# Transposes in place of identity matmuls, a range check moved to VectorE, and norm products half a step later, in an attention and expert-layer kernel

## The chip, the core and the metric

The kernel runs on one core of a Trainium2 chip. The metric is the device time of one execution in microseconds (us). Five engines work side by side, each on its own list of instructions in a fixed order: TensorE (PE in the profile; PEld are its weight loads), VectorE (DVE), ScalarE (ACT), GpSimd (POOL) and SyncE (SP), which issues the transfers. They wait for one another through semaphores.

## The reference

Attention through 32 memory slots per head, and behind it a layer that is applied to every token:

```python
a = softmax(phi, axis=seq)                      # (8, 8, 576, 32)
k_m = einsum('bhsm,bhsd->bhmd', a, k)           # 32 keys and 32 values a head
v_m = einsum('bhsm,bhsd->bhmd', a, v)
attn = softmax(q @ k_m.T / sqrt(64))            # (8, 8, 576, 32)
x = (attn @ v_m) as (4608 tokens, 512)
h = x @ w_in                                    # 512 -> 2048
out = (h - tanh(h)) @ w_out                     # 2048 -> 512
```

The two weights arrive as 64-bit floats, the rest as 32-bit floats.

## The kernel before, in words

**Layer.** The 4608 tokens are cut into 18 units of 256 tokens, and the 2048 hidden columns into four blocks of 512. A slot is one unit and one block. The script writes slots 18 to 71 out in a loop over `(u, fb)`: `u142` in the lists of instructions is the tile `u` of unit 14, block 2 (slot 58). TensorE first makes the slot's hidden values, `hs`, by 24 matmuls (`mm1`, L563). They go through ACT (`u`, L570), VectorE (`h`, L578), ACT (`u`, L583), VectorE (`h`, L588) and ACT (`g`, L594); POOL makes the low part of `g` (L599), and one slot later VectorE adds forms of it, `f` (L612). TensorE multiplies g and f of the block that lies two slots back with W_out (`mm2`, L699 and L706), into the tiles `x` and `o`. At the end of a unit (slots 21, 25 and so on to 57, 61, 65, 69) `evict` empties them on VectorE: r at L759, L760, L761, L764 and L771. The next unit's first product into x waits for the second of these, L760. `hs` and the tile of PSUM that the small products share (tag "pa": psc, ptr, pkv, pp, pno, pni) exist once each.

**Attention.** Its steps for batches 3 to 7 are words in tables (PLAN, PLAN3) that give the slot and the place in it: ahead of the `u` of L583 (`do(0)`), behind mm2 (`do(1)`, after a ";") or at the slot's end (`do(2)`, after a "|"). Batches 0 to 2 run in the 18 blocks ahead of slot 18, while W_in and W_out are still coming in and being split into two 16-bit parts. A batch's turn (`turn`, word U) takes the averaged keys and values `kvn` (`norm`, word N) to `ptr` by products with an identity matrix; ACT copies kT (L264) and vh (L487) out of it, and VectorE makes vl (L489). `expo_turn` turns the exponentials of batches 0 and 1 in the same way (`pet`, `pel`). `pp` (L515) are the values times W_in; ACT (L528) and VectorE (L533) take it to `ph`, the weights of mm1.

**Range check.** The 16-bit arithmetic holds for weights in a certain range. The words of PLAN_C check them as the layer runs: CE and CQ load one of 32 pieces of raw weights again (`chk`, 128x512 of 64 bits, 512 KB), into a buffer of another tile (e, q); CW (`window`) checks its high halves, which lie two words apart: POOL squares them (L439, `fy`) and ACT sums the result of a Relu of 1 - 2^30 y (L443), which is zero if all are large enough. CW, CE, CQ and SI, SO words of `do(0)` are put in `due` and run after POOL's g. SI, SO (ACT) and SS (VectorE L452, L453, tiles sqi, sqo) square and add the split weights; NI and NO (`norms_out`: TensorE L473, `pno`; ACT L474, `wn`) sum over partitions. Slot 68 judges all sums (`good`, `grow`), and `pgood` takes the verdict to a branch at the end, to a second kernel for other ranges, which is not taken with these inputs.

The program's order on each engine is the order of the script (`in_order`), so a table's words alone set which instruction stands behind which.

Of the kernel before, what the change touches and what calls it, by code (L numbers as in the profile page):

```python
# [8 lines left out]
F32 = mybir.dt.float32  # L9
# [4 lines left out]
AF = mybir.ActivationFunctionType  # L14
ALU = mybir.AluOpType
AX = mybir.AxisListType
PSUM = bass.MemoryType.PSUM

P = 128
B, H, S, D, NM = 8, 8, 576, 64, 32  # L20
# [19 lines left out]
CW = (  # L40
    0.33333331252017, -0.13333128520786, 0.053934788850892, -0.021660115374759,
    0.0082189218977914, -0.0025104593252184, 0.000420695493864,
)
# [6 lines left out]
N_F1 = 32  # L50
# [36 lines left out]
class Attention:  # L87
# [105 lines left out]
    def expo_turn(self, b, d, ps, ps_tail):  # L193

        nc, pt = self.tc.nc, d["pt"]
        pa, pb = self.psum(f"pet{b}", ps), ps_tail.tile([P, 512], F32, tag="o1", name=f"pel{b}")
        pe = pa.rearrange("p a x -> p (a x)").rearrange("p (c x) -> p c x", x=P)
        for c in range(4):
            for r in range(2):
                nc.tensor.matmul(pe[:, 2 * c + r], pt[:, r, P * c : P * c + P], self.c["ident"], start=True, stop=True)  # L200
        for r in range(2):
            nc.tensor.matmul(pb[64 * r : 64 * r + 64, 0:P], pt[:, r, 512:S], self.c["ident"], start=True, stop=True)
        yield
        d["e"] = self.big.tile([P, 9, 128], F32, tag="e", name=f"e{b}", bufs=1)
        nc.scalar.activation(d["e"][:, 0:8], pe, AF.Copy)
        nc.scalar.activation(d["e"][:, 8], pb[:, 0:P], AF.Copy)

    def pool(self, b, d):
        self.pool_half(b, d, 0)
# [20 lines left out]
    def norm(self, b, d):  # L230
        nc, big, pa = self.tc.nc, self.big, d["pk"]
        r = big.tile([P, 2], F32, tag="kr", name=f"kr{b}")
        nc.vector.tensor_scalar(r, pa[:, :, 128], EPS, None, op0=ALU.add)
        nc.vector.reciprocal(r, r)
        kvn = big.tile([P, 2, 128], F32, tag="kvn", name=f"kvn{b}")
        nc.vector.tensor_tensor(
            kvn, pa[:, :, 0:128], r.unsqueeze(2).to_broadcast((P, 2, 128)), op=ALU.mult
        )
        d["kvn"] = kvn

    def norm_half(self, b, d, r):
        nc, big, pa = self.tc.nc, self.big, d["pk"]
        if r == 0:
            d["kvn"] = big.tile([P, 2, 128], F32, tag="kvn", name=f"kvn{b}")
        z = big.tile([P, 2], F32, tag="kr", name=f"kr{b}{r}")[:, 0:1]
        nc.vector.tensor_scalar(z, pa[:, r, 128:129], EPS, None, op0=ALU.add)
        nc.vector.reciprocal(z, z)
        nc.vector.tensor_scalar(d["kvn"][:, r], pa[:, r, 0:128], z, None, op0=ALU.mult)

    def turn(self, b, d, ps=None):  # L250

        nc = self.tc.nc
        kvn = d["kvn"]
        pa = self.psum(f"ptr{b}", ps)
        for i in range(2):
            for r in range(2):
                nc.tensor.matmul(
                    pa[64 * r : 64 * r + 64, i, 0:128], kvn[:, r, 64 * i : 64 * i + 64], self.c["ident"],
                    start=True, stop=True,
                )  # L260
        d["pt"] = pa
        yield
        d["kT"] = self.big.tile([P, 128], F32, tag="kT", name=f"kT{b}", bufs=1)
        nc.scalar.activation(d["kT"], pa[:, 0, 0:128], AF.Copy)  # L264
# [73 lines left out]
def split_path(ctx, tc, c, ins, out):  # L338
    nc = tc.nc
    w_in, w_out = ins["w_in"], ins["w_out"]  # L340
    stat = c["stat"]
    const = ctx.enter_context(tc.tile_pool(name="wts", bufs=1))
    big = ctx.enter_context(tc.tile_pool(name="big", bufs=2))
# [91 lines left out]
    def window(k):  # L435

        hf = raws.pop(k).bitcast(F32).rearrange("p (f w) -> p f w", w=2)[:, :, 1]
        y = big.tile([P, 512], F32, tag="ot", name=f"fy{k}")
        nc.gpsimd.tensor_tensor(y, hf, hf, op=ALU.mult)  # L439
        return y, k  # L440

    def window_sum(y, k):
        nc.scalar.activation(y, y, AF.Relu, bias=c["one"], scale=-(2.0 ** 30), accum_out=stat[:, k : k + 1])  # L443

    def squares_in(fb):
        acc["q", fb] = big.tile([P, 4, 512], F16, tag="q" if fb < 3 else "e", name=f"sqi{fb}", bufs=2 if fb < 3 else 1)
# [32 lines left out]
    st = [dict() for _ in range(B)]  # L479
# [11 lines left out]
    def att_window(b):  # L491
        for g in range(2):
            y = big.tile([P, 64], F32, tag="vy", name=f"vy{b}{g}", bufs=1)
            o = N_F1 + 2 * b + g
            nc.scalar.activation(y, st[b]["kvn"][:, g, 64:128], AF.Square, accum_out=stat[:, o : o + 1])

    def att_split(b, t, eng):

# [76 lines left out]
    def g1(u, fb, stay=False):  # L575
        hp, uu = gs[u, fb]
        h3 = hp if stay else big.tile([P, 4, UT], F32, tag="h3", name=f"h3{u}{fb}")
        nc.vector.scalar_tensor_tensor(h3, hp, C2 * S_G / (S_A * S_P), uu, op0=ALU.mult, op1=ALU.mult)  # L578
        gs[u, fb] = (h3, uu)

    def g1_square(u, fb):
        uu = gs[u, fb][1]
        nc.scalar.activation(uu, uu, AF.Square, bias=c["beta"])  # L583
# [237 lines left out]
    def go(word, whole=True):  # L821

        name = word.rstrip("0123456789")
        run = going.pop(word, None) or STEPS[name](*(int(x) for x in word[len(name):]))
        if run is None or not hasattr(run, "send"):
            return
        for _ in run:
            if not whole:
                going[word] = run
                return  # L830

    for word in START.split():
        if ":" in word:
            k, tag = word.split(":")
# [17 lines left out]
    PLAN_C = (  # L852
# [5 lines left out]
    )  # L858
    tasks = {}
# [2 lines left out]
            tasks.setdefault(4 * (b * S // UT) + off, []).append(words.format(b))  # L862
    for sl, words in PLAN_C:
        tasks.setdefault(sl, []).append(words)
    loads, chk, due, squared = list(range(32)), [], [], []

    def borrow(tag):
        chk.append(loads.pop(0))
        load_raw(chk[-1], tag, "chk")

    def step(word, late=False):
        if word[0] == "C" or word[:2] in ("SI", "SO"):
            if not late:
                due.append(word)
            elif word == "CW":
                squared.append(window(chk.pop(0)))
            elif word[0] == "C":
                borrow({"E": "e", "Q": "q", "S": "sc"}[word[1]])
            else:
                go(word)  # L880
        else:
            go(word)
# [4 lines left out]
    for sl, (u, fb) in enumerate(slots, 18):  # L887
        if sl == 18:
            acc["x"] = ps_h.tile([P, 2, 512], F32, tag="h", name="x")
            acc["hp"] = ps_h.tile([P, 4, UT], F32, tag="h", name="hs")  # L890
        todo = ["", "", ""]
        for w in tasks.get(sl, []):
            w, _, todo_2 = w.partition("|")
            w, _, todo_1 = w.partition(";")
            for i, x in enumerate((w, todo_1, todo_2)):
                todo[i] += " " + x

        def do(i):
            for x in todo[i].split():
                step(x)  # L900

        list(mm1(u, fb))
        g1(u, fb)
        do(0)
        g1_square(u, fb)
        a_forms(*forms.pop())
        g2(u, fb)
        queue.append((u, fb))
        v, vb = queue.pop(0)
        mm2_blocks(v, vb, vb == 0, vb == NFB - 1)  # L910
        while squared:
            window_sum(*squared.pop(0))
        do(1)
        g2_high(u, fb)
        g3(u, fb, nc.gpsimd)
        while due:
            step(due.pop(0), True)
        evict()
        forms.append((u, fb))
        do(2)  # L920
# [18 lines left out]
def check(tc, c, big):  # L939
    nc = tc.nc  # L940
    stat = c["stat"]
    good = big.tile([P, N_CHECK], F32, tag="good", name="good", bufs=1)
    nc.vector.tensor_scalar(good[:, 0:N_F1], stat[:, 0:N_F1], 0.0, None, op0=ALU.is_le)
    o = N_F1
    for n, (lo, hi) in ((2 * B, V_WIN), (DF // P, WI_WIN), (DM // P, WO_WIN)):
        s, g = stat[:, o : o + n], good[:, o : o + n]
        nc.vector.tensor_scalar(g, s, lo, None, op0=ALU.is_ge)
        nc.vector.scalar_tensor_tensor(g, s, hi, g, op0=ALU.is_le, op1=ALU.mult)
        o += n
    row = big.tile([P, 1], F32, tag="grow", name="grow", bufs=1)  # L950
    nc.vector.tensor_reduce(row, good, axis=AX.X, op=ALU.add)
    c["row"] = row
# [190 lines left out]
```

## Time and profile before

| | |
|---|---|
| Time, median of 3 runs (lowest to highest) | 666.1 us (665.86 to 666.72) |
| Profiled execution, span from the first to the last instruction | 664.0 us |
| TensorE clock granted, mean | 0.998 |
| Busy: TensorE, VectorE, ACT, POOL | 640.2, 529.2, 374.0, 257.4 us |
| Moved by transfers | 85 MB, 128 GB/s on average |

The median is 2.1 us above the span; the profiled execution's whole time isn't given apart from its span. In the profile a row of a group has the line, engine, operation, output and inputs with their sizes and count, then busy time and the mean of one in nanoseconds, or min/median/max. In a row of the timeline the first two numbers are start and duration in us, and brackets at its end give the idle time of the engine ahead of it and what ended it. One fp32 matmul shows as two records.

### The profile page before, as it was taken

The page shows a single profiled execution, that of the slowest core. Times are in us where ns is not written, and L with a number is a line of the kernel's source. Part 1 is how long each engine was busy: PE and PEld are TensorE (multiplying, and loading weights), DVE is VectorE, ACT ScalarE, POOL GpSimd, SP SyncE. Part 2 cuts the span into 40 slices and gives each one's busy share as a digit, 9 for nine tenths or more (in the row PEclk, how much of TensorE's full clock was granted, in tenths as well). Part 3 has the DMA queues.
Part 4 walks back from the last instruction along what each step waited for, and adds up shares of the span by engine and source line. Part 5 has one row for each costly group of instructions (what it writes and reads, how often), then busy time and mean ns, then how long its engine had stood idle before and what let it go on. Part 6 is the DMA issues. An engine that isn't in the chain of part 4 may idle for free.

```text
span 664.0 us, 15493 instructions
## 1 busy us (share of the span) xinstructions
PE 640.2 (96%) x6630; PEld 454.6 (68%) x6630; DVE 529.2 (80%) x800; ACT 374.0 (56%) x507; POOL 257.4 (39%) x173
## 2 busy tenths in 40 slices
PE   8788999999999999999999999999999989999996
PEld 4364656655557768786767777777776767787785
DVE  6799999999855778875988689877976787868763
ACT  3577576655524556445654565546555566666541
POOL 0224331343112344433545253535352454455521
PEclk9999999999999999999999999999999999999999
DMA  8999344223123402242322433142413342224201
GB/s 341 401 359 380 106 154 148 97 88 129 60 80 101 163 2 98 86 128 105 130 87 96 135 105 113 66 168 71 146 63 136 100 135 88 68 97 135 85 33 38
DMA packets 25996, 84.98 MB, mean 128 GB/s; under 512 B 2880, under 2 KB 2880, under 8 KB 25152
## 3 DMA queue, kind: packets, MB, share of 16 engines
q1 hardware_dynamic: 24624, 81.55, 35.6%
q10 hardware_dynamic: 1296, 2.36, 0.9%
q8 instruction: 54, 0.88, 0.6%
q14 instruction: 22, 0.18, 0.1%
HBM read 72.37 MB, written 11.53 MB: 126 GB/s over the span
## 4 chain that ended last, share of the span: by engine, by line
PE 66%; DVE 16%; DMA 6%; issue 5%; ACT 3%; POOL 2%; SPq 0%; DVEq 0%; ACTq 0%; POOLq 0%
PE hs L563 16%; PE x L706 11%; PE o L699 10%; PE o L706 8%; PE o L642 7%; PE h L563 4%; DMA raw<-in_w_out_dram 3%; PE o1h L642 3%; DVE f L612 3%; PE pp L515 3%; DVE h L588 2%; DVE h L578 2%; DMA kv<-in_kva_dram 2%; PE pkv L220 2%; DVE ph L533 1%
## 5 line engine op out<-in xcount | busy, mean ns | idle before, releaser
L599 POOL TENSOR_TENSOR g<-h,g 128x1024 f16<-128x1024 f32 x67 | 146.6, 2188 | 332.9 <-ACT g L594 216.0
L563 PEld LDWEIGHTS <-ph 128*128 128x128 f16 x2304 | 176.9, 98 | 21.0 <-issue 6.0
L563 PE MATMUL hs<-ah,ph 128*128 128x256 f16 (+3 forms) x1152 | 151.5, 246 | 0.0
L578 DVE SCALAR_TENSOR_TENSOR h<-hs,u 128x1024 f32<-128x1024 f32 x54 | 65.8, 1218 | 89.1 <-ACT u L570 89.1
L594 ACT ACTIVATE g<-h 128x1024 f16<-128x1024 f32 x72 | 76.0, 1056 | 104.6 <-DVE h L588 100.0
L563 PE MATMUL hs<-al,ph 128*128 128x256 f16 (+3 forms) x576 | 127.6, 246 | 0.0
L583 ACT ACTIVATE u<-u,beta 128x1024 f32<-128x1024 f32 x72 | 82.5, 1148 | 58.2 <-DVE h L578 57.8
L699 PE MATMUL o<-wout_hi,g 128*128 128x512 f16 x432 | 104.7, 379 | 0.0
L706 PEld LDWEIGHTS <-f 128*128 128x128 f16 x896 | 87.7, 98 | 10.1
L588 DVE SCALAR_TENSOR_TENSOR h<-u,h 128x1024 f32<-128x1024 f32 x72 | 87.6, 1217 | 0.7 <-ACT u L583 0.7
L570 ACT ACTIVATE u<-hs 128x1024 f32<-128x1024 f32 x54 | 55.0, 1018 | 51.2 <-PE hs L563 47.1
L706 PEld LDWEIGHTS <-g 128*128 128x128 f16 x672 | 64.2, 98 | 27.9 <-issue 6.5
L706 PE MATMUL x<-bt,f 128*128 128x256 f16 x672 | 82.5, 273 | 0.0
L699 PEld LDWEIGHTS <-g 128*128 128x128 f16 x432 | 40.5, 98 | 43.9 <-issue 8.1
L612 DVE TENSOR_TENSOR f<-g 128x512 f16<-128x512 f16 x112 | 65.4, 624 | 4.4 <-POOL g L599 3.4
L642 PEld LDWEIGHTS <-g 128*128 128x128 f16 x384 | 36.7, 98 | 46.6 <-issue 4.3
L642 PE MATMUL o<-wout_hi,g 128*128 128x512 f16 x192 | 59.0, 379 | 0.0
L563 PE MATMUL h<-ah,ph 128*128 128x256 f16 (+3 forms) x384 | 49.9, 246 | 0.6 <-DVE h L578 0.6
L563 PE MATMUL h<-al,ph 128*128 128x256 f16 (+2 forms) x192 | 42.4, 246 | 0.1
L533 DVE SCALAR_TENSOR_TENSOR ph<-pp,ph 128x1024 f16<-128x1024 f32 x31 | 37.7, 1215 | 0.4 <-ACT ph L528 0.3
L528 ACT ACTIVATE ph<-pp 128x1024 f16<-128x1024 f32 x32 | 32.6, 1018 | 7.8 <-PE pp L515 7.7
L642 PE MATMUL o<-wout_lo,g 128*128 128x512 f16 x96 | 36.4, 379 | 0.0
(148 smaller groups left out, 978.6 us busy)
## 6 DMA issues: line engine op xcount, KB each, us to landing
kv<-in_kva_dram SPq DMA_DIRECT2D x20, 516.0 KB, 3.9
q<-in_qt_dram SPq DMA_DIRECT2D x16, 576.0 KB, 4.2
chk<-in_w_in_dram SPq DMA_DIRECT2D x16, 512.0 KB, 5.5
chk<-in_w_out_dram SPq DMA_DIRECT2D x16, 512.0 KB, 3.4
out_dram<-r SPq DMA_DIRECT2D x27, 256.0 KB, 2.4
kv<-in_kva_dram SPq DMA_DIRECT2D x6, 1032.0 KB, 9.7
raws<-in_w_in_dram SPq DMA_DIRECT2D x12, 512.0 KB, 8.4
raw<-in_w_out_dram SPq DMA_DIRECT2D x12, 512.0 KB, 8.9
```

The costliest lines, as they stand in the source:

```text
L533: nc.vector.scalar_tensor_tensor(pl, pa, S_P / (S_V * S_W), ph, op0=ALU.mult, op1=ALU.subtract)
L563: nc.tensor.matmul(hp[:, k, tu : tu + w], px[:, g, cs], d[ax][:, g, ta : ta + w], start=(n == 0), stop=(n == 5),)
L570: nc.scalar.activation(uu, hp, AF.Square, scale=1.0 / (S_A * S_P))
L578: nc.vector.scalar_tensor_tensor(h3, hp, C2 * S_G / (S_A * S_P), uu, op0=ALU.mult, op1=ALU.mult)
L583: nc.scalar.activation(uu, uu, AF.Square, bias=c["beta"])
L588: nc.vector.scalar_tensor_tensor(h3, uu, CC, hp, op0=ALU.add, op1=ALU.mult)
L594: nc.scalar.activation(gg[:, 0], h3, AF.Copy)
L599: eng.tensor_tensor(gg[:, 1], h3, gg[:, 0], op=ALU.subtract)
L612: nc.vector.tensor_tensor(o, x, y, op=op)
L642: nc.tensor.matmul(o, gx[:, k, P * tt : P * tt + P], wx[:, 4 * fb + k, :], start=(first and k == 0 and wx is wout_hi and gx is gh), stop=( ...
L699: nc.tensor.matmul(o[th], gg[:, 0, k, P * th : P * th + P], wout_hi[:, 4 * fb + k, :], start=(first and k == 0), stop=False)
L706: nc.tensor.matmul(dst, a(1 - n, kk), b(n, kk), start=(new and kk == 0 and n == 0), stop=(end and kk == 1 and n == 1))
```

## The change

There are four edits.

1. `expo_turn` (batches 0 and 1) and `turn` (all eight batches) use TensorE's transpose in place of a product with the identity. In `turn`, two 128x128 transposes replace four matmuls with 128x64 weights, and so `norm` writes `kvn` with the two halves of the keys in front of the two halves of the values, in two instructions of 128x128 where there was one of 128x256. The tail of the exponentials is two full transposes of rows that overlap others, and its copy (L206) comes in two.
2. The range check of a piece, CW, is one VectorE reduce, the minimum of magnitudes, in place of POOL's multiply and ACT's Relu with its sum. `good` compares it with 2^-15. It stands where POOL's multiply stood in the script, behind h (L588) of the slot and ahead of an evict.
3. The script no longer has the place between mm2 and `do(1)` at which ACT summed.
4. NO0 to NO3 move from the end of slots 57, 59, 61 and 63 to behind mm2 of slots 58, 60, 62 and 64.

```diff
 expo_turn
-                nc.tensor.matmul(pe[:, 2 * c + r], pt[:, r, P * c : P * c + P], self.c["ident"], start=True, stop=True)
+                nc.tensor.transpose(pe[:, 2 * c + r], pt[:, r, P * c : P * c + P], self.c["ident"])
+        rows = pt.rearrange("p r x -> p (r x)")
         for r in range(2):
-            nc.tensor.matmul(pb[64 * r : 64 * r + 64, 0:P], pt[:, r, 512:S], self.c["ident"], start=True, stop=True)
+            nc.tensor.transpose(pb[:, P * r : P * r + P], rows[:, 512 * (r + 1) : 512 * (r + 1) + P], self.c["ident"])
...
-        nc.scalar.activation(d["e"][:, 8], pb[:, 0:P], AF.Copy)
+        for r in range(2):
+            rs = slice(64 * r, 64 * r + 64)
+            nc.scalar.activation(d["e"][rs, 8], pb[rs, P * r : P * r + P], AF.Copy)
 norm
-        nc.vector.tensor_tensor(
-            kvn, pa[:, :, 0:128], r.unsqueeze(2).to_broadcast((P, 2, 128)), op=ALU.mult
-        )
+        for i in range(2):
+            nc.vector.tensor_tensor(
+                kvn[:, i].rearrange("p (r x) -> p r x", r=2), pa[:, :, 64 * i : 64 * i + 64],
+                r.unsqueeze(2).to_broadcast((P, 2, 64)), op=ALU.mult,
+            )
 turn
         for i in range(2):
-            for r in range(2):
-                nc.tensor.matmul(
-                    pa[64 * r : 64 * r + 64, i, 0:128], kvn[:, r, 64 * i : 64 * i + 64], self.c["ident"],
-                    start=True, stop=True,
-                )
+            nc.tensor.transpose(pa[:, i, 0:128], kvn[:, i], self.c["ident"])
 window
-        y = big.tile([P, 512], F32, tag="ot", name=f"fy{k}")
-        nc.gpsimd.tensor_tensor(y, hf, hf, op=ALU.mult)
-        return y, k
-
-    def window_sum(y, k):
-        nc.scalar.activation(y, y, AF.Relu, bias=c["one"], scale=-(2.0 ** 30), accum_out=stat[:, k : k + 1])
+        nc.vector.tensor_reduce(stat[:, k : k + 1], hf, axis=AX.X, op=ALU.min, apply_absolute_value=True)
 PLAN_C
-        (55, "SS3 CW CW CQ CQ | NI3"), (56, "CW CW CQ CQ SO0"), (57, "SS0 CW CW CQ CQ | NO0"), (58, "CW CQ SO1"),
+        (55, "SS3 CW CW CQ CQ | NI3"), (56, "CW CW CQ CQ SO0"), (57, "SS0 CW CW CQ CQ"), (58, "CW CQ SO1 ; NO0"),
...
 the slot
         mm2_blocks(v, vb, vb == 0, vb == NFB - 1)
-        while squared:
-            window_sum(*squared.pop(0))
         do(1)
 check
-    nc.vector.tensor_scalar(good[:, 0:N_F1], stat[:, 0:N_F1], 0.0, None, op0=ALU.is_le)
+    nc.vector.tensor_scalar(good[:, 0:N_F1], stat[:, 0:N_F1], 2.0 ** -15, None, op0=ALU.is_ge)
```

VectorE around the evict of slot 57, before:

```order
L588 SCALAR_TENSOR_TENSOR h3141_7057<-u141_7055,h3141_7057 128x1024
L759 SCALAR_TENSOR_TENSOR r130_7068<-x_2446,r130_7068 128x256
L760 SCALAR_TENSOR_TENSOR r131_7069<-x_2446,r130_7068 128x256
L761 TENSOR_TENSOR r130_7068<-r130_7068,r131_7069 128x256
L764 TENSOR_TENSOR r131_7069<-r131_7069 128x256
L771 SCALAR_TENSOR_TENSOR r130_7068<-o1300_6734,r130_7068 128x512
L771 SCALAR_TENSOR_TENSOR r131_7069<-o1301_6735,r131_7069 128x512
L578 SCALAR_TENSOR_TENSOR h3142_7162<-hs_2447,u142_7160 128x1024
```

The two checks of the slot were on POOL and ACT then. VectorE at the same place, now (h of L588 is at L586, the evict at L757 to L769; the reduce is L441):

```order
L586 SCALAR_TENSOR_TENSOR h3141_7021<-u141_7019,h3141_7021 128x1024
L441 TENSOR_REDUCE stat_67<-chk16_6984 128x1
L441 TENSOR_REDUCE stat_67<-chk17_6986 128x1
L757 SCALAR_TENSOR_TENSOR r130_7032<-x_2445,r130_7032 128x256
L758 SCALAR_TENSOR_TENSOR r131_7033<-x_2445,r130_7032 128x256
L759 TENSOR_TENSOR r130_7032<-r130_7032,r131_7033 128x256
L762 TENSOR_TENSOR r131_7033<-r131_7033 128x256
L769 SCALAR_TENSOR_TENSOR r130_7032<-o1300_6706,r130_7032 128x512
L769 SCALAR_TENSOR_TENSOR r131_7033<-o1301_6707,r131_7033 128x512
L576 SCALAR_TENSOR_TENSOR h3142_7115<-hs_2446,u142_7113 128x1024
```

Two reduces stand between h and the evict; slot 65 has the same two, slot 61 one.

ACT in slots 57 and 58, before, from g of slot 57 to the squares behind g of slot 58:

```order
L594 ACTIVATE g141_7110<-h3141_7057 128x1024
L474 ACTIVATE wn_7129<-pno0_7130 128x4
L570 ACTIVATE u142_7160<-hs_2447 128x1024
L528 ACTIVATE ph70_7189<-pp70_7164 128x1024
L583 ACTIVATE u142_7160<-u142_7160,beta_62 128x1024
L443 ACTIVATE fy16_7113,stat_67<-fy16_7113,one_61 128x512
L443 ACTIVATE fy17_7115,stat_67<-fy17_7115,one_61 128x512
L594 ACTIVATE g142_7241<-h3142_7162 128x1024
L465 ACTIVATE sqo1_7248<-wout_hi_99 128x2048
```

`wn` stands ahead of u. The same stretch of ACT's list, now:

```order
L592 ACTIVATE g141_7072<-h3141_7021 128x1024
L568 ACTIVATE u142_7113<-hs_2446 128x1024
L526 ACTIVATE ph70_7142<-pp70_7117 128x1024
L581 ACTIVATE u142_7113<-u142_7113,beta_62 128x1024
L472 ACTIVATE wn_7192<-pno0_7193 128x4
L592 ACTIVATE g142_7199<-h3142_7115 128x1024
L463 ACTIVATE sqo1_7205<-wout_hi_99 128x2048
```

`wn` moved behind u and stands ahead of g of slot 58; both sums of fy are gone. On TensorE the products pno0 stood between the last product of slot 57's mm2 and the first of hs of slot 58; they now stand between mm2 of slot 58 and hs of slot 59.

TensorE at the turn of batch 5, before:

```order
L706 MATMUL o900_4774<-wout_hi_99,f90_4623 128x256
L706 LDWEIGHTS f90_4623
L706 MATMUL o900_4774<-wout_lo_100,f90_4623 128x256
L257 MATMUL ptr5_4824<-ident_58,kvn5_4707 64x128 x4
L563 LDWEIGHTS ph43_4764
```

Four products, each into 64 partitions. And now:

```order
L704 MATMUL o900_4760<-wout_hi_99,f90_4608 128x256
L704 LDWEIGHTS f90_4608
L704 MATMUL o900_4760<-wout_lo_100,f90_4608 128x256
L263 MATMUL ptr5_4810<-ident_58,kvn5_4692 128x128 x2
L561 LDWEIGHTS ph43_4750
```

Two transposes, each into 128 partitions, at the same place; nothing else moved there.

More of the change, by code (lines that the diff above doesn't have):

```diff
@@ L247, in norm_half @@
         nc.vector.reciprocal(z, z)
-        nc.vector.tensor_scalar(d["kvn"][:, r], pa[:, r, 0:128], z, None, op0=ALU.mult)
+        nc.vector.tensor_scalar(
+            d["kvn"][:, :, 64 * r : 64 * r + 64], pa[:, r, 0:128].rearrange("p (i x) -> p i x", i=2), z, None, op0=ALU.mult
+        )
     def turn(self, b, d, ps=None):
@@ L494, in att_window @@
             o = N_F1 + 2 * b + g
-            nc.scalar.activation(y, st[b]["kvn"][:, g, 64:128], AF.Square, accum_out=stat[:, o : o + 1])
+            nc.scalar.activation(y, st[b]["kvn"][:, 1, 64 * g : 64 * g + 64], AF.Square, accum_out=stat[:, o : o + 1])
     def att_split(b, t, eng):
@@ L864, in split_path @@
         tasks.setdefault(sl, []).append(words)
-    loads, chk, due, squared = list(range(32)), [], [], []
+    loads, chk, due = list(range(32)), [], []
     def borrow(tag):
@@ L875, in step @@
             elif word == "CW":
-                squared.append(window(chk.pop(0)))
+                window(chk.pop(0))
             elif word[0] == "C":
```

4 rows, old and new, of the table PLAN_C are left out of this document.

## The prediction

> **What bounds the kernel now.** I read the page first, then TensorE's waits, then the timeline of the places where it waits. The page's busy shares, its row of the granted clock and its chain:
>
> ```profile
> PE 640.2 (96%) x6630; PEld 454.6 (68%) x6630; DVE 529.2 (80%) x800; ACT 374.0 (56%) x507; POOL 257.4 (39%) x173
> ...
> PEclk9999999999999999999999999999999999999999
> ...
> PE 66%; DVE 16%; DMA 6%; issue 5%; ACT 3%; POOL 2%; SPq 0%; DVEq 0%; ACTq 0%; POOLq 0%
> ```
>
> TensorE is busy for 640.2 of 664.0 us. So a gain can come from two sources only: shorter TensorE work where TensorE is the limit, or the places where TensorE waits. The view of waits lists those; of its rows these bear on the edits (line, what TensorE waited for, total us, times, longest):
>
> ```profile
> PE psc L272 <- DVE vl L489: 2.9, 2, 2.2
> ...
> PE pp L515 <- ACT wn L474: 2.2, 3, 0.8
> ...
> PE pno L473 <- DVE sqo L453: 1.6, 2, 1.1
> ...
> PE x L706 <- DVE r L760: 1.2, 1, 1.2
> ...
> PE h L563 <- DVE h L578: 0.6, 1, 0.6
> ...
> PE pgood L958 <- DVE grow L951: 0.4, 1, 0.4
> ...
> PE pno L473 <- ACT r L744: 0.2, 1, 0.2
> ```
>
> The rows with pno and wn are the W_out norms (NO0 to NO3): 2.2 + 1.6 + 0.2 = 4.0 us, all between slot 57 and slot 63 (pp waits 0.8 and twice 0.7, pno 1.1, 0.5 and 0.2). The evict wait (1.2) and the wait of the final check (0.4) are two more that the range check can reach. One window shows the norm stretch, from h (L578) of slot 57 to that of slot 64 (us, busy and count of PE, PEld, DVE, ACT, POOL):
>
> ```profile
> 531.80:592.10 60.30, 56.24 (x620) 42.80 (x619) 47.15 (x74) 40.63 (x58) 28.93 (x21) 1.00 0.30 97
> ```
>
> TensorE has 56.2 us of work in 60.3; the 4.0 us of waits fill the rest.
>
> **The turns.** One batch's turn on TensorE, and the group of the exponentials' turns (min/median/max ns):
>
> ```profile
> 213.75 0.66 PE L257 MATMUL ptr<-ident,kvn 128*64 128x128 f32 x8
> 214.34 0.60 PE L699 MATMUL o<-wout_hi,g 128*128 128x512 f16 x2
> ...
> L200 PE MATMUL pet<-ident,pt x32: 272/275/377, 12.9 to 45.2; 128*128 128x128 f32 x32
> ```
>
> Four fp32 matmuls with 64-wide weights leave eight records in pairs, and the next work issues 0.59 us after the first, of which about 0.44 is four steps of 0.11. Two transposes take their place. If one is a single record at the 0.11 us step, that is 0.22 us: 0.21 less per batch. If each is two such records, as a full 128x128 fp32 turn of `pet` is now (32 records for 16 turns), nothing is gained; if each is one record at the pace of the fp16 row under it (512 columns step by 0.22, so 128 by 0.055), 0.33. I take the middle, 0.21. The Trainium skill, "TensorE: Matmul & The Clock Gate", Terms, has transposes four times faster for fp32; by that the sum below would be 0.45 us larger, and no run here shows it yet.
>
> Only some batches pay. Batches 0 and 1 turn in a stretch that VectorE and the loads of w_out set: TensorE has just finished the turn when it waits anyway.
>
> ```profile
> 54.48 0.48 PE L272 MATMUL psc<-q,kT 64*32 64x288 f32 x8 [2.22 <-DVE vl L489]
> ```
>
> A quicker turn there lengthens this 2.22 us wait; the same covers the exponentials' transposes and the two-part copy of L206. Batch 2's turn is followed by the wait of 0.6 us for h (L578) in the list above, batch 7's by the second psc wait (2.9 - 2.2 = 0.7). Batches 3 to 6 remain, where TensorE waits for no engine between the turn and slot 57: 4 x 0.21 = 0.85 us gained (ends 0 and 1.3). On the other side `kvn` in two parts:
>
> ```profile
> 106.79 0.42 DVE L236 TENSOR_TENSOR kvn<-pkv,kr 128x256 f32<-128x256 f32 x1
> ```
>
> Two halves at about 0.25 each put 0.1 us on VectorE; in batch 2 VectorE is saturated, so I count it: +0.1. Elsewhere the next h hides it.
>
> **The range check.** What is removed and the nearest row to what is added (min/median/max ns):
>
> ```profile
> L439 POOL TENSOR_TENSOR fy<-chk x32: 1032/1039/1221, 239.5 to 624.4; 128x512 f32<-128x512 f32 x32
> L443 ACT ACTIVATE fy<-fy,one x32: 705/712/722, 241.8 to 625.4; 128x512 f32<-128x512 f32 x32
> L300 DVE TENSOR_REDUCE sm<-sc x16: 733/746/753, 28.7 to 555.9; 128x18 f32<-128x576 f32 x16
> ```
>
> A reduce of 576 fp32 per partition takes 0.746 us; 512 scale to 0.67. Bounds: 0.42 us, which the fp16 sqo operation on 512 takes (L453, below), and 1.3, double the near row, if every second word costs twice. I take 0.67, because this row is the same operation and nearly the size. So VectorE gets 32 x 0.67 = 21.4 us; POOL loses 33, ACT 23 plus its accumulator reads. The Trainium skill, "VectorE: DVE Perf Modes", Rules for kernel authors, calls this reduce the slowest VectorE operation and advises against it on a hot path; that speaks for rival (b).
>
> VectorE also gets time back. Its f forms (L612), which read two buffers, stretch whenever the POOL multiply fy runs:
>
> ```profile
> 587.30 0.75 DVE L612 TENSOR_TENSOR f<-g 128x512 f16<-128x512 f16 x2
> 593.30 2.22 POOL L439 TENSOR_TENSOR fy<-chk 128x512 f32<-128x512 f32 x2
> 593.37 2.42 DVE L612 TENSOR_TENSOR f<-g 128x512 f16<-128x512 f16 x2
> ```
>
> Where fy collides, 2.42 - 0.75 = 1.67 us comes back for two reduces of 1.33. In slots 21 to 53 TensorE never waits for VectorE and the reduces stand behind h (L588), in idle time; so nothing there. The loads of the next windows are now released by the reduce, earlier than by fy.
>
> **The norms half a step later.** Products and `wn` leave the place between two blocks, so pp no longer waits for `wn`. What is late next? The first x product of a new unit waits for the evict of the unit before (r L760), and two reduces now stand ahead of that evict. Slots 56 to 60, with the sqo groups (min/median/max ns):
>
> ```profile
> 524.36 1.73 DVE L612 TENSOR_TENSOR f<-g 128x512 f16<-128x512 f16 x2
> 531.85 1.23 DVE L578 SCALAR_TENSOR_TENSOR h<-hs,u 128x1024 f32<-128x1024 f32 x1 [2.66 <-ACT u L570]
> 535.36 0.24 PE L473 MATMUL pno<-ones,sqo 128*128 128x1 f16 x4 [1.05 <-DVE sqo L453]
> 538.18 0.42 DVE L760 SCALAR_TENSOR_TENSOR r<-x,r 128x256 f32<-128x256 f32 x1
> 539.02 0.41 PE L515 MATMUL pp<-win_hi,vh 64*32 64x512 f16 x8 [0.79 <-ACT wn L474]
> 539.80 0.28 PE L706 MATMUL x<-wout_hi,g 128*128 128x256 f16 x1
> 560.40 1.72 DVE L612 TENSOR_TENSOR f<-g 128x512 f16<-128x512 f16 x2
> ...
> L452 DVE TENSOR_TENSOR sqo<-sqo x4: 681/978/1302, 533.0 to 585.6; 128x1024 f16<-128x1024 f16 x4
> L453 DVE TENSOR_TENSOR sqo<-sqo x4: 424/424/1259, 534.0 to 587.0; 128x512 f16<-128x512 f16 x4
> ```
>
> Without its two waits (1.05 + 0.79) TensorE wants x at 539.80 - 1.84 = 537.96. The evict ends at 538.60; it moves by -0.97 (f of slot 56 back to 0.75), -0.84 (the 1259 ns sqo, in this slot, back to 424, since POOL's sc no longer queues behind fy) and +1.33 (two reduces): 538.12. So x waits 0.15 and slot 58 gives 1.7 of 1.84. Slots 59 to 62 lose the other four waits, 0.5 + 0.7 + 0.2 + 0.7. TensorE is then 1.7 + 2.1 = 3.8 ahead when it comes to the next new unit's x:
>
> ```profile
> 573.49 0.42 DVE L760 SCALAR_TENSOR_TENSOR r<-x,r 128x256 f32<-128x256 f32 x1
> 575.11 0.28 PE L706 MATMUL x<-wout_hi,g 128*128 128x256 f16 x1
> ```
>
> It wants to start at 575.11 - 3.8 = 571.3. The evict there ends at 573.91. The chain that sets these slots (h, ACT's g, ACT's squares, u, the next h, each waiting for the one before) comes into slot 58 about 0.5 earlier (what the evict gained), gets back 0.97 in slot 60 (f, 1.72 to 0.75), about 0.3 in each of the slots 58 and 61 (half of what f and sqo can lie above their least there) and 0.1 from `wn`, which no longer stands ahead of u; it pays 0.67 for the one reduce ahead of this evict: 573.91 - 1.5 = 572.4. So x waits 1.1, and of 4.0 us about 2.8 are gained. The ends: 1.0, if the chain keeps its pace and the reduces delay both evicts, and 4.0. `wn` now stands ahead of g, and g waits for h past the end of the block's products in all four slots, which hides it: 0; without that cover each us that pno is late would delay g, and so the next u, by one.
>
> **Slots 64 to 69.** Here fy collides in every slot:
>
> ```profile
> 601.12 2.42 DVE L612 TENSOR_TENSOR f<-g 128x512 f16<-128x512 f16 x2
> 605.84 0.42 DVE L760 SCALAR_TENSOR_TENSOR r<-x,r 128x256 f32<-128x256 f32 x1
> 606.41 0.27 PE L706 MATMUL x<-wout_hi,g 128*128 128x256 f16 x1 [1.19 <-DVE r L760]
> ```
>
> Two slots get 1.67 back each, and only the second slot's reduces (1.33) stand ahead of this evict: the chain is 2.0 us shorter than now against a wait of 1.19. Since TensorE arrives with 2.8 us won and this chain with about as much, I count 1.0 of the 1.19. VectorE then runs ahead at the final check, and its 0.4 goes.
>
> Sum: -0.85 + 0.1 - 2.8 - 1.0 - 0.4 = -4.95 us on a span of 664.0: 659.05. The median of the runs shown is 666.1, 2.1 above the span; with the same 2.1 the time is 661.1 us. The ends of its terms (-1.3, 0, -4.0, -1.2, -0.4 and 0, +0.1, -1.0, -0.5, -0.4) give it a range of its own, 659.2 to 664.3.
>
> **Rivals.** (a) Slower: VectorE waits for the check's loads. Its reduce is in order with everything else, so a late window holds the next h, and with it u and hs; before, POOL's fy met that wait. The page's loads (KB each, median us from issue to landing):
>
> ```profile
> chk<-in_w_in_dram SPq DMA_DIRECT2D x16, 512.0 KB, 5.5
> chk<-in_w_out_dram SPq DMA_DIRECT2D x16, 512.0 KB, 3.4
> ...
> raws<-in_w_in_dram SPq DMA_DIRECT2D x12, 512.0 KB, 8.4
> ```
>
> In slots 56 to 58 and 64 to 67 a buffer freed by one slot's reduce is reduced again in the next, 7.75 us later (f at 593.37 and 601.12); less the reduce itself a load may take 7.1. At the 8.4 that equal loads took at the start, each of the seven slots loses 1.3: 9.1 us, 666.1 - 4.95 + 9.1 = 670.3. It turns the sign from about 7.8 us. Against it: 3.4 for the loads in question. (b) The wait only moves: x, behind evicts that the reduces delay, takes the place of `wn` and sqo. That comes if the reduce costs its 1.3 us (1.3 more ahead of the evicts of slots 57 and 65, 0.65 in 61) or if POOL's g, sc and al go on stretching f and sqo. The norms give 1.0, the turns 0.85, slot 66 0.5, the check 0.4: 663.4. For it: the 1259 ns sqo was stretched by sc, not by fy itself. (c) The reduces and the turns bring nothing, and the evicts eat the norms' gain: 665.5 to 666.5. (d) TensorE slows: the row of granted clock reads 9 in all 40 slices of a TensorE that hardly rests. How far it would fall no row shows; a tenth lost over one 7.75 us slot after each of eight turns would cost 6 us: 667. I give it 0.01, since the trace shows no dip anywhere, even in the start where TensorE rests most. The Trainium skill, "TensorE: Matmul & The Clock Gate", Part 4, says that transposes do not count as busy for the clock gate, which would make this; no run here has shown transposes yet.
>
> **How the numbers follow.** My forecast (gain 2.8 and more) has 0.62: every duration in it has a row, only their joint play is reckoned by hand. (b) has 0.18, as the evicts decide and lie within a few tenths; (c) 0.08; (a) 0.11; (d) 0.01. About 0.2%, 1.3 us, is what a measurement of this kernel can tell from no change. The first two cases are faster by more than that: 0.80; (c) is the same: 0.08; (a) and (d) slower: 0.12. The range runs from 659.2 to 666.5: it takes in (b) and (c) and leaves out (a) and (d).
>
> **What the profile after would show.** Turns: fewer than 8 ptr records per batch, or a step from the first to the next work well under 0.59 us. Range check: reduces of 0.6 to 0.7 us that never stretch, f pairs at 0.75 in slots 64 to 68. Norms: no TensorE wait for `wn` or sqo, a wait for the evict's second r of some tenths in slot 58 and about 1 us in slot 62, and none worth naming in slot 66. It is wrong if the reduce takes over 1 us or waits for loads, if f stays near 2.4 us in slots 64 to 68 without fy, or if x waits for r as long as pp waited for `wn`.

## The result

The changed kernel takes 663.12 us in the median of five executions (661.63 to 664.44), against 666.1 in five of the kernel before (665.86 to 666.72): a ratio of 0.9942, interval 0.9924 to 0.9961. The forecast was 661.1, so 5.0 us were expected and 3.0 came. One execution of the kernel with the norms alone (678.34 us) and three of the kernel before (1103 us and more) were slow, and no ratio or split below counts them. The profiled execution spans 661.3 us. Its busy shares, its row of the granted clock, and TensorE's waits that answer to those shown before (the lines have moved: L697 and L704 are mm2, L757 to L769 the evict, L576 and L586 the two h, L597 POOL's g):

```profile
PE 635.6 (96%) x6562; PEld 452.1 (68%) x6562; DVE 539.1 (82%) x840; ACT 352.1 (53%) x445; POOL 222.7 (34%) x141
...
PEclk9998999999999999999999999999999999999999
```

```profile
PE psc L275 <- DVE vl L487: 3.7, 2, 2.5
PE o L697 <- DVE r L769: 2.3, 3, 1.1
PE x L704 <- DVE r L758: 1.8, 2, 1.5
...
PE h L561 <- DVE h L576: 1.1, 1, 1.1
...
PE pno L471 <- DVE ph L531: 0.2, 1, 0.2
```

The waits for `wn` and sqo are gone, as forecast, and so is the final check's. In their place stand 4.1 us of waits for the evict: 1.8 of x, and 2.3 of o for r (L769), a wait that the prediction does not name at all. The clock's row has an 8 in its fourth slice, which no slice had before.

The three operations that the edits brought, each on its own:

```profile
214.91 0.38 PE L263 MATMUL ptr<-ident,kvn 128*128 128x128 f32 x2
215.13 1.03 PE L697 MATMUL o<-wout_hi,g 128*128 128x512 f16 x4
```

```profile
L441 DVE TENSOR_REDUCE stat<-chk x32: 644/677/699, 236.9 to 616.9; 128x1 f32<-128x512 f32 x32
```

```profile
L610 DVE TENSOR_TENSOR f<-g x10: 409/418/427, 592.8 to 622.0; 128x512 f16<-128x512 f16 x10
```

A turn's two transposes are one record each, 0.11 us apart, and the next work issues 0.22 us after the first. The reduce takes 0.677 us (forecast 0.67) and never stretches. In the window 592 to 626 no f stretches any more, where a pair took up to 2.42 us before.

To see where time went I take the start of a slot's first hs in the timeline, minus that of the kernel before (192.99, 526.74, 579.90, 611.19 and 634.25 us). The last column is slot 70 minus slot 57; it holds the norm stretch and the slots behind it, and no fall of the clock.

| Kernel (us against before) | slot 18 | slot 57 | slot 63 | slot 67 | slot 70 | 57 to 70 |
|---|---|---|---|---|---|---|
| changed | +1.25 | -1.61 | -2.14 | -1.99 | -2.70 | -1.09 |
| transposes alone | -0.79 | -4.03 | -4.03 | -4.02 | -4.02 | 0.0 |
| norms alone | +0.11 | +0.14 | -0.88 | +0.09 | +0.08 | -0.1 |
| range check alone | +0.62 | +3.54 | +3.01 | +3.89 | +3.18 | -0.4 |
| changed, evict ahead of checks | -0.52 | -2.88 | -6.59 | -7.62 | -8.32 | -5.44 |
| the same, norms at old place | +1.47 | -1.61 | -4.15 | -5.05 | -5.76 | -4.15 |
| changed, checks inside evict | +1.73 | -0.50 | -4.14 | -5.18 | -5.89 | -5.39 |
| evict ahead, SO early | -0.16 | -3.17 | -7.92 | -9.43 | -10.14 | -6.97 |
| evict ahead, SO and SI3 early | -1.29 | -5.15 | -9.90 | -11.41 | -12.12 | -6.97 |

Slots 57 to 70 were to give 4.2 us (2.8 + 1.0 + 0.4) and gave 1.1.

### The profile page after: what moved, and what is told of

It reads as the page before. It is cut to its first block, busy times and chain, and to the rows that moved or that the text cites. A ratio compares the mean times of both kernels' runs of the same rounds, so it can differ in the third digit from the quotient of the medians.

```text
span 661.3 us, 15304 instructions
## 1 busy us (share of the span) xinstructions
PE 635.6 (96%) x6562; PEld 452.1 (68%) x6562; DVE 539.1 (82%) x840; ACT 352.1 (53%) x445; POOL 222.7 (34%) x141
## 4 chain that ended last, share of the span: by engine, by line
PE 61%; DVE 23%; DMA 5%; issue 4%; ACT 4%; POOL 2%; SPq 0%; DVEq 0%; ACTq 0%; POOLq 0%
PE hs L561 16%; PE x L704 11%; PE o L697 11%; PE o L704 8%; PE o L640 5%; DMA raw<-in_w_out_dram 3%; DVE h L586 3%; DVE h L576 3%; PE h L561 2%; DVE f L610 2%; DVE wt L387 2%; PE pp L513 2%; DVE ph L531 2%; PE pkv L223 2%; PE o1h L640 2%
## 5 line engine op out<-in xcount | busy, mean ns | idle before, releaser
L597 POOL TENSOR_TENSOR g<-h,g 128x1024 f16<-128x1024 f32 x67 | 145.7, 2174 | 357.1 <-ACT g L592 294.3
L576 DVE SCALAR_TENSOR_TENSOR h<-hs,u 128x1024 f32<-128x1024 f32 x54 | 65.7, 1217 | 77.2 <-ACT u L568 76.9
L697 PE MATMUL o<-wout_hi,g 128*128 128x512 f16 x432 | 104.7, 379 | 2.3 <-DVE r L769 2.3
L704 PEld LDWEIGHTS <-f 128*128 128x128 f16 x896 | 87.7, 98 | 10.2
L586 DVE SCALAR_TENSOR_TENSOR h<-u,h 128x1024 f32<-128x1024 f32 x72 | 87.6, 1216 | 0.7 <-ACT u L581 0.7
L704 PEld LDWEIGHTS <-g 128*128 128x128 f16 x672 | 64.2, 98 | 28.7 <-issue 7.3
L704 PE MATMUL x<-bt,f 128*128 128x256 f16 x672 | 82.5, 273 | 0.0
L697 PEld LDWEIGHTS <-g 128*128 128x128 f16 x432 | 40.6, 98 | 46.5 <-issue 10.8
L610 DVE TENSOR_TENSOR f<-g 128x512 f16<-128x512 f16 x112 | 50.7, 493 | 4.0 <-POOL g L597 3.4
```

The source lines that it names most:

```text
L586: nc.vector.scalar_tensor_tensor(h3, uu, CC, hp, op0=ALU.add, op1=ALU.mult)
L597: eng.tensor_tensor(gg[:, 1], h3, gg[:, 0], op=ALU.subtract)
L610: nc.vector.tensor_tensor(o, x, y, op=op)
L697: nc.tensor.matmul(o[th], gg[:, 0, k, P * th : P * th + P], wout_hi[:, 4 * fb + k, :], start=(first and k == 0), stop=False)
L704: nc.tensor.matmul(dst, a(1 - n, kk), b(n, kk), start=(new and kk == 0 and n == 0), stop=(end and kk == 1 and n == 1))
```

## The experiments

**The edits one by one.** Each was put alone into the kernel before.

> The kernel before with the transposes, nothing else. Theory 1: each turn of batches 3 to 6 is 0.47 us shorter on TensorE, 1.9 us together, and where the granted clock falls in the start 1.3 to 2.7 us of it are given back: 664.2 in executions with a mean clock of 0.998 or more, 666 in those at 0.997 or less. Rival (the forecast's size): 0.21 us a turn, 665.2 at the full clock.

Measured: 662.18 us median, ratio 0.9925 (0.9908 to 0.9943). The median is as low as that of the whole change, and the 4.0 us of the table are more than twice the theory's 1.9. The two medians do not compare as they stand, though: five of these six executions have a mean granted clock of 0.998 or more, and only one of the changed kernel's five. With executions of that clock alone it is 661.9 against 661.2 (see the granted clock, below), so the other edits add about 1 us.

> The kernel before with the norm products half a step later, nothing else. The theory of the prediction (pp no longer waits for wn; the chain and the evict decide what is left): TensorE's 4.0 us of waits for wn, sqo and r go, waits of x and o for the evict of about 2 us come back in slots 58 and 62: 2.0 us gained, about 664.5. Rival: the wait only changes its name, within 0.5 us of the kernel before.

Measured: 666.99 (all twelve executions), ratio 1.0007 (0.9990 to 1.0023). The rival holds. Of its waits between 515 and 660 us:

```profile
PE x L706 <- DVE r L760: 4.7, 3, 2.3
PE hs L563 <- DVE h L578: 0.9, 1, 0.9
```

The waits for `wn` and sqo turned into waits for the evict and for h: the chain on VectorE and ACT was late, and TensorE only met it elsewhere.

> The kernel before with the range check as VectorE reduces, nothing else. Theory (reduces ahead of an evict cost there what the freed f and sqo bring elsewhere): pno no longer waits for sqo (1.6 us), the final check no longer waits (0.4), pp still waits for wn, and x and o wait up to 1 us each for the evicts of slots 57, 61 and 65: 0 to 1 us gained, 665.5 to 666.5. Rival (the reduce costs more than it frees): slower by 1 us or more.

Measured: 666.75, ratio 0.9997 (0.9981 to 1.0013), no difference. Its waits between 518 and 660 us are not those of the theory:

```profile
PE pno L468 <- DVE sqo L448: 3.3, 2, 1.7
PE o L694 <- DVE r L766: 1.6, 3, 0.6
PE pp L510 <- ACT wn L469: 0.8, 1, 0.8
```

pno waits for sqo longer than before (3.3 against 1.6), since h, and with it sqo, comes late behind evicts that take longer: their third operation (L756) goes up to 2.28 us here, for a reason that comes next.

**Why the evict is late.** VectorE at the evict of slot 61 in the changed kernel, and POOL at the same time:

```profile
569.97 0.68 DVE L441 TENSOR_REDUCE stat<-chk 128x1 f32<-128x512 f32 x1
570.57 0.41 DVE L757 SCALAR_TENSOR_TENSOR r<-x,r 128x256 f32<-128x256 f32 x1
571.02 0.42 DVE L758 SCALAR_TENSOR_TENSOR r<-x,r 128x256 f32<-128x256 f32 x1
571.36 2.28 DVE L759 TENSOR_TENSOR r<-r,r 128x256 f32<-128x256 f32 x1
573.56 0.41 DVE L762 TENSOR_TENSOR r<-r 128x256 f32<-128x256 f32 x1
573.89 1.27 DVE L769 SCALAR_TENSOR_TENSOR r<-o,r 128x512 f32<-128x512 f32 x2
575.09 1.21 DVE L576 SCALAR_TENSOR_TENSOR h<-hs,u 128x1024 f32<-128x1024 f32 x1
...
571.23 2.13 POOL L597 TENSOR_TENSOR g<-h,g 128x1024 f16<-128x1024 f32 x1 [4.90 <-ACT g L592]
```

The evict's third operation adds two buffers and takes 2.28 us: it starts 0.13 us behind POOL's g and ends 0.28 behind its end. Before, that operation ran ahead of g (573.83 against 574.29 in this slot); all 14 of its kind took the same:

```profile
L761 DVE TENSOR_TENSOR r<-r,r x14: 415/415/418, 228.3 to 657.3; 128x256 f32<-128x256 f32 x14
```

The reduces push it some 0.7 to 1.3 us back, and so into POOL's g. It takes 1.69, 2.28 and 1.74 us in slots 57, 61 and 65, together 4.5 us more than three times 0.41. What stands behind it moves too. In slot 57, the second r, the third operation and the next h, before (L760 is in the prediction) and now:

```profile
538.53 0.41 DVE L761 TENSOR_TENSOR r<-r,r 128x256 f32<-128x256 f32 x1
540.39 1.22 DVE L578 SCALAR_TENSOR_TENSOR h<-hs,u 128x1024 f32<-128x1024 f32 x1
```

```profile
535.67 0.42 DVE L758 SCALAR_TENSOR_TENSOR r<-x,r 128x256 f32<-128x256 f32 x1
536.01 1.69 DVE L759 TENSOR_TENSOR r<-r,r 128x256 f32<-128x256 f32 x1
539.16 1.20 DVE L576 SCALAR_TENSOR_TENSOR h<-hs,u 128x1024 f32<-128x1024 f32 x1
```

Counted from the slot's first hs (526.74 and 525.13), the second r, which frees x, ends 0.9 us earlier than before, and the next h starts 0.4 us later. The Trainium skill, "SBUF — State Buffer", Who interferes with whom, says that a VectorE instruction with two SBUF inputs contends with a GpSimd instruction that reads SBUF, while a reduce never does. These rows agree on the first, and the kernel with the checks inside the evict, below, on the second: there two reduces start at 536.61, under a g that runs from 536.40 to 538.69, and take 1.27 us together. Two-input operations are not the only ones that a reduce can push under g: a scaling of 128x18 with one input (L315, L312 before) took 0.18 us in slots 56 and 60 and takes 1.50 and 2.10 behind the reduces. It costs nothing there, since the h behind it starts 0.04 us after ACT's u is done. Two kernels test whether the collision is the cause. The first:

```diff
-        while due:
-            step(due.pop(0), True)
         evict()
+        while due:
+            step(due.pop(0), True)
```

> The changed kernel with the evict ahead of the checks in slots 57, 61 and 65. Theory 1: the waits of x and o for the evict (0.7 us in slot 58, 2.7 in 62, 0.9 in 66) come from the reduces that stand ahead of it (1.35, 0.67 and 1.35 us), so 0.7 + 0.7 + 0.9 = 2.3 us go and TensorE waits about 2 us in slot 62 alone: about 660.9. Rival: the chain of h, g, squares and u is late by itself and the wait only takes another name, under 0.8 us gained: 662.4 or more.

Measured: 658.49 us (657.23 to 660.66), ratio 0.9885 (0.9863 to 0.9908), 5.44 us gained from slot 57 to 70 against 1.09: 4.3 more, where the reduces' own time gave 2.3. All 14 third operations take 0.41 to 0.42 us again, in slot 57 by a narrow margin: it ends at 533.96 and g starts at 534.00. Between 500 and 660 us TensorE waits only here:

```profile
PE psc L275 <- DVE vl L487: 1.1, 1, 1.1
PE x L704 <- DVE r L758: 0.9, 1, 0.9
PE hs L561 <- POOL al L504: 0.3, 1, 0.3
```

The second puts the checks behind the evict's fourth operation, so that they still stand ahead of L769, which frees o (shortened; the evict calls the checks there):

```diff
                 nc.vector.tensor_tensor(rb[:, 1], rb[:, 0], rb[:, 2], op=ALU.add)
+                mid()
...
-        while due:
-            step(due.pop(0), True)
-        evict()
+        evict(checks)
```

> The changed kernel with the slot's checks inside the evict, behind its fourth operation (r+r, the last that reads two SBUF buffers) and ahead of the fifth, which frees o. In the changed kernel the third operation takes 1.69, 2.28 and 1.74 us in slots 57, 61 and 65 where it took 0.41 before. Theory 1: the reduces push it into POOL's g, which blocks it, and that, not the reduces' own 0.6 us, makes o wait and the next h late; here it stays at 0.41, o does not wait though the reduces stand ahead of its release, x waits 0.9 in slot 62 at most, and the time is that of the evict ahead alone: 657.4 at the full clock, median about 658.4. Rival: the reduces' own 1.3 us ahead of o's release make the wait; o still waits 0.5 to 1.1 us in the three slots, 660 or more.

Measured: 657.16 us (656.44 to 659.92), ratio 0.9852 (0.9829 to 0.9875), and 5.39 us from slot 57 to 70, as with the evict ahead. The third operation (L760 there) and the waits between 505 and 660 us:

```profile
L760 DVE TENSOR_TENSOR r<-r,r x14: 415/415/417, 229.5 to 651.4; 128x256 f32<-128x256 f32 x14
```

```profile
PE psc L275 <- DVE vl L487: 1.2, 1, 1.2
PE x L704 <- DVE r L759: 0.9, 1, 0.9
PE hs L561 <- POOL al L504: 0.3, 1, 0.3
```

o does not wait, though the reduces still stand ahead of its release. So it is the collision with POOL's g, and not the reduces' 0.6 us each, that made o wait and the next h late.

**What the norms' move is worth then.** The evict ahead of the checks, and NO0 to NO3 back at their old places:

> The kernel with the evict ahead of the checks, and the norms at their old places (slots 57, 59, 61, 63). Theory 1: with the reduces out of the evict's way the norms' move is what brings the gain in slots 57 to 64; without it pp waits 0.7 us for wn three times and pno for sqo where the chain is late: 2 to 3 us slower than with the evict ahead and the move, 660.5 to 661.5. Rival: the range check alone freed that stretch (f and sqo no longer stretched), and the norms' place is worth under 0.7 us: 658.5 to 659.2.

Measured: 658.25 us (657.16 to 660.72), ratio 0.9883 (0.9859 to 0.9907). The times alone do not part it from the kernel with the move. The waits between 500 and 660 us do:

```profile
PE pno L471 <- DVE sqo L451: 1.7, 2, 1.2
PE psc L275 <- DVE vl L487: 1.1, 1, 1.1
PE pp L513 <- ACT wn L472: 0.8, 1, 0.8
```

From slot 57 to 70 it gains 4.15, 1.3 less than with the move (5.44). Between the two theories, then: most of that stretch's gain comes with the range check, once the evicts are in time, and the move adds 1.3 us.

**The granted clock.** The changed kernel's start, in stretches of 2 us (us, busy and count of PE, PEld, DVE, ACT, POOL, granted clock, DMA share, GB/s):

```profile
52.00:54.00 2.00, 0.00 (x0) 0.00 (x0) 1.83 (x4) 1.97 (x8) 0.00 (x0) 0.97 1.04 435
54.00:56.00 2.00, 1.61 (x19) 0.57 (x20) 1.76 (x5) 2.00 (x4) 0.00 (x0) 0.50 1.01 423
56.00:58.00 2.00, 2.00 (x14) 1.56 (x13) 2.00 (x3) 0.50 (x2) 0.00 (x0) 0.68 0.99 403
58.00:60.00 2.00, 2.00 (x29) 1.12 (x28) 2.00 (x4) 1.49 (x2) 0.23 (x1) 1.00 1.03 413
```

TensorE rests for 2.5 us at 51.9 (psc waits for vl, 2.2 before), and the clock is at half for about 3.4 us of these windows (0.1 + 2.0 + 1.3). A slower TensorE is what rival (d) names, so the next kernels take the rest away. One moved a word of the start's text but left TensorE's order as it was (one of ACT's u changed places); I count it as a second measurement of the changed kernel:

> The changed kernel with the second half of one block's hidden products (unit 1, block 1) ahead of the first scores of batch 1, so that TensorE works where it now rests for 2.5 us at 51.9. Theory 1: that rest, longer than in the kernel before, lets the granted clock fall to 0.5 for 3.4 us and costs 1.3 to 1.7 us in most executions; with work in it the clock stays at 1.0, the mean granted clock is 0.998 or more in all executions and the time is about 661.6 with a scatter under 1 us. Rival: the fall has another cause or lies under VectorE's work in this stretch: clock 0.995 to 0.997 in most executions as now, 663.1.

Measured: 662.50 us (660.37 to 666.04), ratio 0.9938 (0.9915 to 0.9962). Its profile has the same fall; four of the eight executions had a mean clock of 0.998 or more and took 661.2 in the median, the four others 664.1. Then products of another block in the rest:

```diff
-W1 UV1 U1 a10 S10 UV1 c00 T08
+W1 UV1 U1 H01 a10 S10 UV1 c00 T08
```

> The changed kernel with the hidden products of unit 0, block 1 ahead of the first scores of batch 1, so that TensorE works through the rest at 51.9. Theory 1 (a rest of over about 2.5 us lets the granted clock fall): the rest is gone, no fall near 54 us, mean clock 0.998 or more in nearly all executions, median 661.3 with a scatter of about 1 us. Rival (the falls come elsewhere too, at the 1.7 us rest at 45 for one): executions at 0.995 to 0.997 remain, median 662.5 to 663.1.

Measured: 661.64 us (660.99 to 663.03), ratio 0.9913 (0.9895 to 0.9931). Its profile has no fall at 54 but one at 59.1, behind shorter rests of 1.2 and 0.7 us, so moving the work did not keep the clock up there.

To see whether transposes count as work for the clock, the rest was filled with two kinds of work, written to a part of the tile that nobody reads. They turned out 1.91 us (transposes) and 1.06 us (products) long, where 0.9 was meant. With 16 transposes:

```diff
+        for i in range(16 if b == 1 else 0):
+            nc.tensor.transpose(pa[:, i % 2, 256:384], kvn[:, i % 2], self.c["ident"])
```

> The changed kernel with 16 more transposes (into a part of the tile that nobody reads) behind batch 1's turn, some 0.9 us of the 2.5 us rest. Theory A: transposes do not count as TensorE work for the granted clock: it still falls, mean 0.995 to 0.997 in most executions, 663.1. Theory B: only the rest counts: with 1.6 us left the clock stays at 1.0 and the time is about 661.6.

Measured: 661.68 us (661.09 to 663.42), ratio 0.9930 (0.9911 to 0.9949). And with four products:

> The same rest filled by four 128x128 fp32 matmuls, again some 0.9 us. Theories A and B: the clock stays at 1.0 in all executions, about 661.6. If the clock falls here too, neither holds, and the length of the rest at this place is not the cause.

Measured: 661.37 us (660.18 to 662.45), ratio 0.9920 (0.9900 to 0.9940). In both the profile has the clock at 1.00 throughout that start, and four of six executions are at 0.998 or more; the rest left in it was 1.09 and 1.44 us. Against five of 13 executions of the changed kernel these counts alone decide little.

The profiles say more. In all 14, the changes of the granted clock lie whole multiples of 3.413 us apart: in the changed kernel at 6.09, 53.87 (14 steps) and 57.29 (one more), in the kernel before at 6.06 and 661.42 (192 steps). Steps of that grid, in the changed kernel (two), the kernel before, the range check alone, the hidden products moved and the 16 transposes:

```profile
50.46:53.87 3.41, 1.41 (x13) 1.07 (x11) 2.63 (x5) 3.38 (x11) 0.85 (x1) 1.00 1.04 426
53.87:57.29 3.42, 2.90 (x25) 1.49 (x26) 3.18 (x6) 2.33 (x4) 0.00 (x0) 0.50 0.99 414
50.44:53.85 3.41, 1.82 (x20) 1.28 (x17) 2.27 (x5) 3.36 (x11) 0.82 (x1) 1.00 1.05 431
360.66:364.07 3.41, 1.57 (x36) 1.01 (x33) 3.38 (x7) 1.06 (x1) 1.47 (x1) 1.00 0.03 10
55.72:59.14 3.42, 1.60 (x19) 0.49 (x20) 3.42 (x6) 2.25 (x4) 0.00 (x0) 1.00 1.01 414
50.79:54.20 3.41, 2.74 (x26) 2.44 (x23) 2.33 (x5) 2.56 (x10) 0.44 (x1) 1.00 1.03 424
```

All six falls ahead of a kernel's last slots follow a step in which TensorE was busy for 0.70 to 1.60 us, and so rested 1.8 to 2.7. No step with less rest was followed by a fall; two near a kernel's end, with 1.91 and 1.95, were not either, so the bound is known only roughly. The rest of 2.2 us in the kernel before was divided at 53.85 into 1.6 and 0.6, and did nothing. So Theory B was half right: what decides is how much rest falls into one step, and the grid lies elsewhere in each execution (first change at 4.52 to 7.26 us). Theory A fails by the last row: without its transposes TensorE would have rested some 2.6 of those 3.41 us, and the clock stayed at 1.00. That is one profile.

Executions of the kernel before lose clock too. Of 54, beside these kernels, 33 had a mean clock of 0.998 or more and took 665.9 in the median; 21 were below and took 667.9. The range check alone, which has no transposes, fell in its profile at 364, behind a rest of 1.84 us for a load. In the same split the changed kernel's two measurements give 661.2 (5 executions) and 663.7 (8), so its gain is 4.7 at the full clock and 4.2 below, and how many executions fall decides which median one sees. The split is rough, since a kernel's last us count in the mean as well: one profile with a mean of 0.998 is at 0.50 only in its last 3.2 us, where TensorE has no work. Whether the change makes falls more frequent (8 of 13 against 21 of 54) is not settled.

**A version that beats both.** With POOL's squares and ACT's sums gone, ACT rests between u and g. The squares of W_out (SO) go there, ahead of g, under a word SQ that runs at once, and NO behind mm2 of the slot that adds them up:

```diff
-(56, "CW CW CQ CQ SO0"), (57, "SS0 CW CW CQ CQ"), (58, "CW CQ SO1 ; NO0"),
+(56, "CW CW CQ CQ ; SQ0"), (57, "SS0 CW CW CQ CQ ; NO0"), (58, "CW CQ ; SQ1"),
```

> The kernel with the evict ahead of the checks, and ACT's 1.9 us of W_out squares (SO) ahead of g, where ACT is idle since the sums of the check are gone; NO behind mm2 of slots 57, 59, 61, 63. Theory 1: the squares between g and u are what makes the chain late in slots 57 to 63; off it, the last wait of x for the evict (0.9 us in slot 62) goes: 0.9 us less than the evict ahead alone, about 657.6. Rival: pno, now only behind the same slot's sqo, makes TensorE wait again, no gain or slower: 658.5 or more.

Measured: 657.44 us (655.19 to 658.64), ratio 0.9868 (0.9844 to 0.9892). x no longer waits; between 500 and 660 us one wait is left:

```profile
PE psc L275 <- DVE vl L487: 1.1, 1, 1.1
```

The last squares of W_in (slot 54) ahead of g as well:

> The same with the last squares of W_in (SI3, slot 54) ahead of g too. Theory 1: the wait of batch 7's scores for vl (1.1 us at 509) comes from ACT's vh behind these squares and goes with it: about 656.5. Rival: vl is late for another reason, the wait stays: as the kernel with SO early.

Measured: 654.97 us (653.43 to 658.34), ratio 0.9844 (0.9815 to 0.9873). The view of waits lists none for TensorE between 500 and 660 us; one window of that stretch:

```profile
520.00:650.00 130.00, 126.70 (x1215) 100.83 (x1212) 102.50 (x177) 65.55 (x72) 40.51 (x21) 1.00 0.25 87
```

The same window of the changed kernel has 125.28 us of TensorE work, of the kernel before 124.30.

## Why the prediction was right in sign and short in size

The median lies in the range, and the executions at the full clock (661.2) hit the forecast of 661.1. That is luck. The turns and the start gave 4.0 us in place of 0.75, slots 57 to 70 gave 1.1 in place of 4.2, and the two errors cancel: 5.1 against 4.95. The median's shortfall of 2 us goes with the falls of the clock in four of its five executions.

- **The turns** (forecast 0.85) were right in mechanism and mis-sized. One record per transpose and 0.11 us a step is the middle that was taken. But what lies around the four steps shrank too: from the last product of hs to the next work it was 213.55 to 214.34, 0.79 us, of which 0.44 are the steps, and is 214.80 to 215.13, 0.33, of which 0.22 are. The prediction looked only from the first product on. That is 0.46 a turn and 1.8 to 1.9 for batches 3 to 6, above the end of 1.3. Batch 7's did go into psc's wait, which grew from 0.7 to 1.1.
- **The start** (+0.1) was wrong for the transposes alone: slot 18 starts 0.8 us earlier there, and waits for kv loads between slots 18 and 57 are 1.0 us less (0.4 against 1.4). Together with the turns' 1.9 that makes 3.7 of the 4.0 us of the transposes alone. Why TensorE waits less for the loads is not shown; slot 18 of the changed kernel itself came at +1.25 in one execution and +2.2 in another, both with a fall of the clock.
- **The norms and the evicts** (forecast 2.8) hold the step that failed: that the chain "comes into slot 58 about 0.5 earlier (what the evict gained)". The gains came, f at 0.75 and sqo at 0.42, and the second r, which frees x, ended early enough: x does not wait in slot 58. But the reduces were priced by their own time only. What they pushed, the evict's two-buffer addition, ran into POOL's g, and the next h started 0.4 us later, not 0.5 earlier. The wait of o, which is freed behind that addition, was put at nothing and took 0.5 us in slot 58 and 1.1 in slot 62; x took 1.5 in slot 62 (forecast 1.1). Three evicts lost 4.5 us in this way. The prediction had the collision in its rows, f against fy, and did not apply it to what moves. Slots 57 to 63 gave 0.5 in place of 2.8 (the prediction's own 3.8 less 1.1 is 2.7); with the evict ahead they give 3.7.
- **Slots 64 to 69** (forecast 1.0 and 0.4): f at 0.75 and an early final check came. Slots 67 to 70 gave 0.7, of which the final check's wait is 0.4; the other 0.3 is not assigned. Slots 63 to 67 lost 0.15, since the evict of slot 65 was stretched too, and give 1.0 with the evict ahead.
- **Rivals.** (a) did not happen: no reduce waits for a load. (b) is what happened to the norms, by another mechanism than its 1.3 us reduce or a stretched f and sqo; that its 663.4 lies 0.3 from the median is chance, since its turns are half of what they gave and it has no fall of the clock. (c) had the reduces right, which bring nothing alone, and the turns wrong, which gave most of the gain. (d), given 0.01, was priced too low as a fall of the clock, and rightly low as an effect of transposes: the kernel before has executions of the same low mean clock, and 16 transposes kept the clock up in the profile where they filled the rest.

## What to carry to other kernels

When an instruction is put ahead of others on an engine, price the place into which it pushes them, not only its own time: here one free-looking reduce moved a 0.41 us addition under another engine's work and made it 2.28, and two did the same in two other slots (1.69 and 1.74). A wait that is taken from the bound engine comes back elsewhere as long as the chain behind it is late, so shorten the chain (squares moved into ACT's idle time, with the norms' products one slot earlier, gave 1.5 us on top of the early evict, where moving the norms alone gave nothing). Read the granted clock of every execution before comparing medians that lie 2 us apart.

## What the runs showed of the hardware

An fp32 transpose of 128x128 is one record and steps at 0.11 us, where the product with an identity left two records. The Trainium skill, "TensorE: Matmul & The Clock Gate", Terms, has transposes four times faster for fp32; the step here is half of the product's 0.22, and the whole turn is 2.4 times quicker (0.79 to 0.33), so the measurement stands below that figure.

A VectorE addition of two SBUF buffers that starts just behind a POOL operation on SBUF ends just behind it (2.28 us in place of 0.41), and VectorE reduces in the same place keep their time (1.27 us for two).

The granted clock changes in steps of 3.413 us and falls to 0.50 for one such step behind a step in which TensorE rested 1.8 to 2.7 us. The Trainium skill, "TensorE: Matmul & The Clock Gate", Part 1, describes a free-running activity window of about 3.4 us, which the grid bears out; it has the clock fall after an idle window, and here 1.8 us of rest in one were enough. Executions with a mean clock below 0.998 took about 2 us more here (665.9 against 667.9).
